# Gated linear attention feeding a mixture of experts: the order of the first loads and TensorE's first products

## The chip, the cores and the metric

The kernel runs on one core of one Trainium2 chip. The metric is the device time of one execution in microseconds (us), smaller is better. Engines are named as the profile names them: PE is TensorE's matmul, PEld its weight load, DVE is VectorE, ACT ScalarE, POOL GpSimd, and SP the engine that only issues transfers; a trailing q (SPq, ACTq) is an engine's sequencer, where the issue of a transfer is shown.

## The reference

The inputs are q, k, v and f_logit of shape (4, 8, 768, 48) in fp32. Attention is a gated recurrence per batch and head, and its rows go through a router to one of eight experts:

```python
f = 1.0 / (1.0 + np.exp(-f_logit))
for t in range(S):
    state = f[:, :, t, :, None] * state + np.einsum('bhd,bhe->bhde', k[:, :, t], v[:, :, t])
    y[:, :, t] = np.einsum('bhd,bhde->bhe', q[:, :, t], state)
x = y.transpose(0, 2, 1, 3).reshape(B * S, H * D)      # 3072 rows of 384
logits = x @ w_gate; e = argmax(logits)                # 8 experts
# the first `capacity` rows of an expert go through relu(x @ w1[e]) @ w2[e],
# scaled by the softmax of their gate
```

## The kernel before, in words

Attention works through 24 chunks of 128 tokens (six for each of the four batches), all eight heads of a chunk at once, heads paired two by two. A chunk n is taken through these steps, named by the function and the line that the profile shows:

- `load` (L205, L210, L216) issues its transfers from SP: "f" for two chunks at once (384 KB), k and q of one chunk (192 KB each, k on partitions 0 to 63, q on 64 to 127), v (192 KB). f, kq and v have 3, 3 and 6 buffers. Only the first half of f's first load is split over SP and ACT (L214), heads 0 to 3 and heads 4 to 7.
- `sig` (L357, ACT) applies the sigmoid to a load of f; for the first load rows 0 to 63 and rows 64 to 127 are done apart.
- `f_in` (L366, PE) transposes f of a chunk, eight transposes per chunk. `decay` (L386, L394, L395, DVE) is a scan backwards over it, `decay_back` (L400, DVE) a scan forwards.
- `kq_pad` (L407, POOL up to chunk 9, then ACT) copies k and q into a padded tile, `kq_in` (L366, PE; L415, DVE) transposes them and multiplies the transposes by the two scans to give kT and qT.
- `scores_pe` (L426, PE), `scores_out` (L432 ACT, L434 POOL) make the masked scores AT; `keys_pe` and `keys_out` (L451, L457) the key rows; `inter` (L468) the part from the state S; `update` (L488), `state` (L502 or, for a first chunk, L500, DVE) and `carry` (L508, POOL) the next state; `values` (L522) the part from the scores; `y_out` (L534) and `rows_pe` (L543) turn the output into rows, and `rows_copy` (L559) and `rows_parts` (L569) put them and their logits into `ring`, a tile of 12 chunks of rows. From slot 7 on, a group's expert choice is ranked and POOL scatters its rows to `disp` in DRAM (L326), one chunk of rows in a slot.

The order on all five engines is the order of emission, written out by hand: `prologue` (L770) takes chunk 0 and the first steps of chunks 1 to 3, and `slot(n)` (L826) then holds, for one n, the scores of chunk n+1, kq_in of n+2, the decay of n+3, the loads of later chunks (`loads_of`, L812) and the values of chunk n. `keep_busy(m)` (L373) is m products of the identity with itself into a PSUM tile that nobody reads; a fp32 product shows as two matmul instructions, a transpose as one. There are 7 of them before the first transposes, 4 before kq_in(0) and 2 before kq_in(1).

`late_constants` (L278) loads the gate weights into `identc` with four transfers of 32-byte pieces, issued by SP behind the load of v for chunk 1. `zero_disp` (L345) writes 393 KB of zeros to `disp`, once for each of two regions, in slots 1 and 3, ahead of any scatter; each scatter must come behind both, since its rows can fall in either.

After attention (from about 150 us) the experts run as dense products (L754, L1015, L1222), each expert's weights loaded during the one before.

Of the kernel before, what the change touches and what calls it, by code (L numbers as in the profile page):

```python
# [9 lines left out]
F32 = mybir.dt.float32  # L10
# [4 lines left out]
AF = mybir.ActivationFunctionType  # L15
# [5 lines left out]
P = 128  # L21
# [8 lines left out]
def kernel(  # L30
# [12 lines left out]
    nc = tc.nc  # L43
    B, H, S, D = q.shape
    N, DM = out.shape
    NE = w_gate.shape[1]
    DF = w1.shape[2]
    NP = H // 2
    HALF = 384
    C = 128  # L50
# [3 lines left out]
    R = 64 + D  # L54
    DT = DM // P
    FT = DF // P
    W = DM + NE + 1
# [4 lines left out]
    RT, RING = 4, 12  # L62
# [20 lines left out]
    psT = ctx.enter_context(tc.tile_pool(name="psT", bufs=2, space=PSUM))  # L83
    psA = ctx.enter_context(tc.tile_pool(name="psA", bufs=2, space=PSUM))
# [5 lines left out]
    ident = const.tile([P, P], F32, name="ident")  # L90
# [81 lines left out]
    actx = ExitStack()  # L172
    apool = actx.enter_context(tc.tile_pool(name="apool", bufs=1))
    abuf = actx.enter_context(tc.tile_pool(name="abuf", bufs=2))
    raw0 = actx.enter_context(tc.tile_pool(name="raw0", bufs=3))
    h0pool = actx.enter_context(tc.tile_pool(name="h0pool", bufs=1))

# [2 lines left out]
    loads, pf, kqp = {}, [], []  # L180
    for nm in ("f", "kq", "v"):
        for i in range(NLOAD[nm]):
            if nm == "v":
                t = apool.tile([P, H, 64], F32, name=f"ld_{nm}{i}")
                nc.gpsimd.memset(t[:, :, D:], 0.0)
            else:
                t = apool.tile([P, H, 2, D], F32, name=f"ld_{nm}{i}")
            loads[nm, i] = t
    for made, nm, n in ((pf, "pf", 2), (kqp, "kqp", 2)):
        for i in range(n):  # L190
            t = apool.tile([P, 2, H, 64], F32, name=f"{nm}{i}")
# [7 lines left out]
    def load(nm, n):  # L199
        if n >= (NT // 2 if nm == "f" else NT):  # L200
            return
        t = loads[nm, n % NLOAD[nm]]
        if nm == "v":
            b, t0 = n // CPB, n % CPB * C
            nc.sync.dma_start(t[:, :, :D], srcs[nm][b, :, t0 : t0 + C, :].rearrange("h p d -> p h d"))  # L205
            return
        t = t.rearrange("t h j d -> t h (j d)")
        if nm == "kq":
            for h, x in enumerate(nm):
                nc.sync.dma_start(t[64 * h : 64 * h + 64], pairs(x, n, C))  # L210
        elif n == 0:
            for h, queue in enumerate((nc.sync, nc.scalar)):
                hs = slice(4 * h, 4 * h + 4)
                queue.dma_start(t[:64, hs], pairs(nm, 0, C)[:, hs])  # L214
        else:
            nc.sync.dma_start(t, pairs(nm, 2 * n, 2 * C))  # L216

    def loaded(nm, n):
        return loads[nm, n % NLOAD[nm]]

    for nm, n in (("f", 0), ("kq", 0), ("kq", 1), ("f", 1), ("kq", 2), ("v", 0), ("f", 2)):
        load(nm, n)
        if (nm, n) == ("kq", 0):
            nc.sync.dma_start(loads["f", 0].rearrange("t h j d -> t h (j d)")[64:], pairs("f", 1, C))
# [5 lines left out]
    for i in range(2):  # L230
        t = apool.tile([P, NP * C], F32, name=f"Suf{i}")
# [21 lines left out]
    for g in range(2):  # L253
        r = slice(64 * g, 64 * g + D)
# [23 lines left out]
    def late_constants():  # L278
        gates_of = w_gate.rearrange("(a b s d) e -> b s d a e", b=2, s=2, d=D)
        for g in range(2):  # L280
            for b in range(2):
                nc.sync.dma_start(identc[64 * g : 64 * g + D, b::2, 2 * D :], gates_of[b, g ^ b])
    ohc = const.tile([P, NE], BF16, name="ohc")
    lt = const.tile([P, NS, NS], F32, name="lt")
    put_off(nc.gpsimd.memset, lt, 1.0)
# [59 lines left out]
    def zero_disp(v):  # L345
        ins = nc.sync.dma_start(
            disp[v * RPE : v * RPE + 2 * P, :].rearrange("(a p) w -> p a w", p=P),
            zero.unsqueeze(1).broadcast_to([P, 2, W]),
        )
        after(ins, pace["ins"], "behind the first loads")  # L350

    def sig(u):
        if u >= NT // 2:
            return
        cuts = (0, 64, P) if u == 0 else (0, P)
        for r0, r1 in zip(cuts, cuts[1:]):
            pace["ins"] = nc.scalar.activation(  # L357
                pf[u % 2][r0:r1, :, :, :D], loaded("f", u)[r0:r1].rearrange("t h j d -> t j h d"), AF.Sigmoid
            ).ins

    def transposes(*dsts):
        for p in range(NP):
            for j in range(2):
                for t, src, h in dsts:
                    r = slice(64 * h, 64 * h + 64)
                    nc.tensor.transpose(  # L366
                        t[:R, p, j::2], src[r, j, 2 * p : 2 * p + 2].rearrange("t s d -> t (s d)")[:, :R], ident[r, r]
                    )
        return [t[:R].rearrange("r p t -> r (p t)") for t, src, h in dsts]

    Fs, Rqs, kTs, qTs = {}, {}, {}, {}

    def keep_busy(m):  # L373
        pw = psA.tile([P, P], F32, name="psA")
        for _ in range(m):
            nc.tensor.matmul(pw, ident, ident, start=True, stop=True)  # L376

    def f_in(*ns):
        made = [(psF.tile([P, NP, C], F32, name="psF"), pf[n // 2 % 2], n % 2) for n in ns]
        for n, F in zip(ns, transposes(*made)):  # L380
            Fs[n] = F

    def decay(n):
# [19 lines left out]
    def kq_pad(n):  # L403
        if n < NT:
            src = loaded("kq", n).rearrange("t h j d -> t j h d")
            if n - 3 < PAD_ACT:
                nc.gpsimd.tensor_copy(kqp[n % 2][:, :, :, :D], src)  # L407
            else:
                nc.scalar.activation(kqp[n % 2][:, :, :, :D], src, AF.Copy)

    def kq_in(n):
        pts = transposes(*((psT.tile([P, NP, C], F32, name="psT"), kqp[n % 2], h) for h in range(2)))
        for nm, pt, by, made in (("kT", pts[0], Sufb[n % 2], kTs), ("qT", pts[1], Rqs.pop(n), qTs)):
            t = abuf.tile([P, NP, C], F32, name=nm, bufs=3)
            nc.vector.tensor_tensor(t[:R].rearrange("r p t -> r (p t)"), pt, by[:R], op=ALU.mult)  # L415
            made[n] = t
# [120 lines left out]
    def rows_pe(n):  # L537
        yT = yTs.pop(n)
        px = psA.tile([P, NP, XW], F32, name="psA")
        for p in range(NP):  # L540
            for t in range(2):
                ts = slice(64 * t, 64 * t + 64)
                m_pe = nc.tensor.matmul(px[ts, p, :], yT[:R, p, ts], identc[:R, p, :], start=True, stop=True)  # L543
        marks[n] = [m_pe]
        return px

    ring = abuf.tile([P, RING, W], F32, name="rows", bufs=1)

    def row_at(n):
        return ring[:, n % RING]  # L550
# [136 lines left out]
    def flush_scatter():  # L687
        if queue:
            n = queue.pop(0)
            late = n >= SPLIT  # L690
            ins = scatter(disp, ri_of.pop(n), row_at(n), NV * RPE - 1, ("disp", "late") if late else ("disp",))
            if not late:
                early_ins[:] = [ins]
# [74 lines left out]
    slots = range(NT + 1)  # L768

    def prologue():  # L770
        keep_busy(7)
        nc.scalar.activation(warm, direv[:, :1], AF.Sigmoid)
        sig(0)
        f_in(0)
        decay_back(0, decay(0))
        kq_pad(0)
        load("kq", 3)
        load("v", 1)
        late_constants()
        keep_busy(4)  # L780
        kq_in(0)
        f_in(1)
        decay_back(1, decay(1))
        kq_pad(1)
        later_ops(put_off_ops)
        keep_busy(2)
        kq_in(1)
        sig(1)
        kq_pad(2)
        pas = scores_pe(0)  # L790
        f_in(2)
        decay_back(2, decay(2))
        scores_out(0, pas)
        pks = keys_pe(0)
        keys_out(0, pks)
        f_in(3)
        load("kq", 4)
        load("v", 2)
        load("kq", 5)
        load("f", 3)  # L800
    ends = {g + m - 1: (g, m) for g, m in GROUPS}

    def rank(g, pool):
# [8 lines left out]
    def loads_of(n):  # L812
        load("v", n + 3)
        if 0 < n < PAD_ACT:
            load("kq", n + 6)
        if n == 0:
            load("f", 4)
        if n == 2:
            nc.sync.dma_start(cap_i, capacity.bitcast(I32).partition_broadcast(P))
        if n in (1, 3):  # L820
            zero_disp(0 if n == 1 else NE)
        for k, at in enumerate(PIECE_LOAD):
            if at == n:
                pieces[k] = weight_piece(wsets[0], 0, raw0, k)

    def slot(n):  # L826
# [17 lines left out]
            choose_first(*half.pop())  # L844
        for g in full:
            choose_sum(*g)
        if n == 1:
            f_in(4)
        if kqn:
            kq_in(n + 2)  # L850
        if n % 2 and fn and n not in (1, 9, 15):
            f_in(n + 3, n + 4)
        if nxt:
            scores_out(n + 1, pas)
        if n == 0:
            sig(2)
        if prev and cur and first(n):
            y_out(n - 1)
# [31 lines left out]
        if nxt:  # L890
            for s in range(SCATTERS.get(n, 2)):
                flush_scatter()
        if fn:
            F = decay(n + 3)
        if prev:
            px = rows_pe(n - 1)
            if tail:
                rows_logits(n - 1, px)
                rows_copy(n - 1, px)
                chosen[n - 1] = choose_one(row_at(n - 1), abuf, tallies[-1][:, 1:2]), 1  # L900
            else:
                rows_copy(n - 1, px)
                rows_parts(n - 1, px)
# [587 lines left out]
```

## Time and profile before

| | us |
|---|---|
| three timed runs | 374.07, 376.09, 376.36 (median 376.09) |
| the profiled execution | 375.17 |
| its span, first to last instruction | 373.40 |
| around the span | 1.77 |
| mean granted TensorE clock of the span | 0.990 |

The span is the part that the views below cut up. A row of a timeline or of the chain has a start, a duration and an instruction group; "[0.34 <-PE psT L366]" is the idle time of that engine just before it, and what ended it. The durations of matmuls overlap, since their ends are modelled; in the chain each has only its own share.

### The profile page before, as it was taken

The numbers are of one execution on the slowest core, as the hardware profiler recorded it, in microseconds if no ns is written. First come the engines' busy times: TensorE is split into PE (matmuls) and PEld (weight loads), VectorE is DVE, ScalarE is ACT, GpSimd is POOL, SyncE is SP. The second block draws the span as 40 slices with busy tenths as digits, with TensorE's granted clock in tenths as the row PEclk, the third lists the DMA queues.
The fourth block names the chain that finished last, engine by engine and source line by source line (L and its number), as shares of the span: only waits on it lengthen the run. The fifth ranks groups of instructions, "written<-read, shape, count | busy, mean of one in ns | idle before, by whom it ended". The sixth has DMA issues, their size and how long they took to land.

```text
span 373.4 us, 10082 instructions
## 1 busy us (share of the span) xinstructions
PE 362.1 (97%) x3895; PEld 340.8 (91%) x3895; DVE 247.8 (66%) x533; ACT 223.8 (60%) x458; POOL 166.5 (45%) x275
## 2 busy tenths in 40 slices
PE   8999999999899999999999999999999999999993
PEld 7999898888787889999899999999999999999993
DVE  4898988979687866753676296857757665570300
ACT  3356677877586763255477475759578586583310
POOL 6665556675757675235613702127117244144012
PEclk9999999999899999999999999999999999999997
DMA  8999999999997432476696979799797997721001
GB/s 153 187 177 224 205 207 227 256 214 226 213 227 164 130 114 105 133 237 204 191 239 188 286 196 242 212 187 319 169 204 247 172 208 253 129 94 52 14 23 40
DMA packets 111351, 67.86 MB, mean 182 GB/s; under 512 B 93646, under 2 KB 105844, under 8 KB 111296
## 3 DMA queue, kind: packets, MB, share of 16 engines
q1 hardware_dynamic: 107504, 57.09, 69.1%
q0 software_dynamic: 3520, 9.97, 7.7%
q8 instruction: 32, 0.52, 0.6%
q14 instruction: 23, 0.19, 0.2%
q10 hardware_dynamic: 272, 0.10, 0.1%
HBM read 49.46 MB, written 11.43 MB: 163 GB/s over the span
## 4 chain that ended last, share of the span: by engine, by line
PE 84%; issue 8%; ACT 3%; POOL 2%; DVE 1%; POOLq 1%; ACTq 0%
PE psM L1222 15%; PE psA L754 9%; PE psM L1015 9%; PE psT L754 9%; PE psM L754 7%; PE psA L426 6%; PE psY L522 6%; PE psA L543 5%; PE psT L366 4%; PE psY L468 3%; PE psA L488 3%; PE psT L451 3%; PE psF L366 2%; POOL out_dram L326 2%; PE psA L376 2%
## 5 line engine op out<-in xcount | busy, mean ns | idle before, releaser
L326 POOL DMA_INDIRECT out_dram<-yo,g_ti x30 | 31.3, 1042 | 55.6 <-ACT yo L1019 31.7
L434 POOL TENSOR_SCALAR_AFFINE_SELECT AT<-AT 128x512 f32<-128x512 f32 x48 | 29.4, 637 | 23.3 <-ACT AT L432 23.2
L1015 PE MATMUL psM<-w2h,hh 128*128 128x384 f32 (+2 forms) x112 | 37.5, 340 | 0.0
L1015 PE MATMUL psM<-w2l,hh 128*128 128x384 f32 (+2 forms) x112 | 37.3, 338 | 0.0
L1015 PE MATMUL psM<-w2h,hl 128*128 128x384 f32 (+2 forms) x112 | 37.2, 338 | 0.0
L135 ACT ACTIVATE w2h<-raw 128x768 fp32r<-128x768 f32 x32 | 27.0, 844 | 11.2 <-DMA raw<-in_moe_w_dram 11.2
L1222 PE MATMUL psM<-hh,w2h 128*128 128x440 f32 (+3 forms) x96 | 33.7, 351 | 0.0
L1222 PE MATMUL psM<-hh,w2l 128*128 128x440 f32 (+3 forms) x96 | 33.7, 351 | 0.0
L1222 PE MATMUL psM<-hl,w2h 128*128 128x440 f32 (+3 forms) x96 | 33.6, 350 | 0.0
L144 DVE TENSOR_TENSOR w2l<-raw,w2h 128x768 fp32r<-128x768 f32 x28 | 27.8, 994 | 7.7 <-ACT w2h L135 6.9
L386 DVE TENSOR_TENSOR_SCAN Suf<-psF,direv 112x511 f32<-112x511 f32 x24 | 29.1, 1212 | 4.5 <-PE psF L366 4.5
L432 ACT ACTIVATE AT<-psA 128x512 f32<-128x512 f32 x48 | 26.4, 612 | 8.9 <-PE psA L426 5.6
L1242 POOL COPY yo<-yq 128x384 uint16<-128x384 uint16 (+4 forms) x16 | 11.9, 790 | 40.1 <-DMA yq<-yp 38.2
L426 PE MATMUL psA<-qT,kT 48*128 48x128 f32 x384 | 29.4, 293 | 0.0
L400 DVE TENSOR_TENSOR_SCAN Rq<-psF,d 112x512 f32<-112x512 f32 x24 | 29.4, 1223 | 0.0
L326 POOL DMA_INDIRECT disp<-rows,ri x24 | 24.8, 1034 | 9.5 <-issue 4.3
L144 DVE TENSOR_TENSOR w1l<-raw,w1h 128x1024 fp32r<-128x1024 f32 x21 | 26.5, 1269 | 2.9 <-ACT w1h L135 2.6
L761 DVE SCALAR_TENSOR_TENSOR hl<-psA,hh 128x224 fp32r<-128x224 f32 (+8 forms) x26 | 14.2, 547 | 21.3 <-ACT hh L760 19.3
L559 ACT ACTIVATE rows<-psA 128x384 f32<-128x384 f32 x24 | 11.8, 491 | 26.0 <-PE psA L543 19.6
L522 PE MATMUL psY<-AT,ld_v 128*48 128x128 f32 (+1 forms) x384 | 26.9, 278 | 0.0
L426 PEld LDWEIGHTS psA<-qT,kT 48*128 48x128 f32 x384 | 25.8, 201 | 0.5 <-issue 0.5
L135 ACT ACTIVATE w1h<-raw 128x1024 fp32r<-128x1024 f32 x24 | 24.8, 1060 | 1.9 <-DMA raw<-in_moe_w_dram 1.9
(253 smaller groups left out, 1041.7 us busy)
## 6 DMA issues: line engine op xcount, KB each, us to landing
raw<-in_moe_w_dram SPq DMA_DIRECT2D x24, 512.0 KB
raw<-in_moe_w_dram SPq DMA_DIRECT2D x32, 384.0 KB
ld_kq<-in_k_dram SPq DMA_DIRECT2D x24, 192.0 KB
ld_kq<-in_q_dram SPq DMA_DIRECT2D x24, 192.0 KB
ld_v<-in_v_dram SPq DMA_DIRECT2D x24, 192.0 KB
ld_f<-in_f_logit_dram SPq DMA_DIRECT2D x11, 384.0 KB
xg<-disp SPq DMA_DIRECT2D x6, 589.5 KB
xg<-disp SPq DMA_DIRECT2D x3, 393.0 KB
```

Source lines behind the costliest of these rows:

```text
L135: return nc.scalar.activation(hi, raw, AF.Copy)
L144: engine.tensor_tensor(lo[cs], raw[cs], hi[cs].bitcast(F32), op=ALU.subtract)
L326: ins = nc.gpsimd.indirect_dma_start(out=dst, out_offset=bass.IndirectOffsetOnAxis(ap=idx, axis=0), in_=rows, in_offset=None, bounds_check ...
L386: nc.vector.tensor_tensor_scan(out=_view(Suf[:R], m - 1, [[-1, m]]), data0=_view(F, m, [[-1, m]]), data1=_view(direv[:R], m - 1, [[-1, m]] ...
L400: nc.vector.tensor_tensor_scan(out=Rq[:R], data0=F, data1=d1[:R], initial=0.0, op0=ALU.mult, op1=ALU.max)
L426: nc.tensor.matmul(pas[s][:, p], kTs[n][r, p], qTs[n][r, p], start=True, stop=True)
L432: nc.scalar.activation(AT[:, s], pas[s], AF.Copy)
L434: nc.gpsimd.affine_select(AT[:, s], AT[:, s], pattern=[[0, NP], [1, C]], compare_op=ALU.is_ge, fill=0.0, base=0, channel_multiplier=-1)
L522: nc.tensor.matmul(py[b][64 * g : 64 * g + m, a, :], vt[:, 2 * p + s, :m], AT[:, s, p, :], start=(first(n) and a == 0), stop=(a == NP // 2 ...
L754: nc.tensor.matmul(ph[:, :T], a[:, c, fs], x[:, c, :T], start=(n == 0), stop=(n == 3 * DT - 1))
L1015: nc.tensor.matmul(py[:n], x[:, ks], a[:, ft], start=(ft == 0 and m == 0), stop=(ft == FT - 1 and m == 2))
L1222: nc.tensor.matmul(pys[c][:, :T], a[:, ft, cs], x[:, :T], start=(ft == 0 and n == 0), stop=(ft == FT - 1 and n == 2))
```

## The change

It reserves the tile `ring` earlier, fills 128 x 128 of it with ones on DVE (`hot`) and multiplies that in `keep_busy` instead of the identity, with 8 products at the start in place of 7. Beside the eight transposes of f_in(0), which read partitions 0 to 63, eight more read the ones on partitions 64 to 127 into another PSUM tile. The first sigmoid is cut in two by heads, kq_pad(0) by partitions (k, then q), and kq_in(0) transposes k first and q after it, not in turns. Of the loads, f of chunks 4 and 5 is issued behind k and q of chunk 3, f of chunks 6 and 7 ahead of k and q of chunk 5, the gate weights are issued by ACT, and the two zero_disp move from slots 1 and 3 to slots 4 and 6. The sigmoid for chunks 4 and 5 moves from slot 0 to slot 1, and f_in(4) within slot 1 from ahead of kq_in(3) to behind rows_pe(0).

```diff
+    ring = abuf.tile([P, RING, W], F32, name="rows", bufs=1)
+    hot = ring[:, 0, :P]
+    nc.vector.memset(hot, 1.0)
...
-    for nm, n in (("f", 0), ("kq", 0), ("kq", 1), ("f", 1), ("kq", 2), ("v", 0), ("f", 2)):
+    for nm, n in (("f", 0), ("kq", 0), ("kq", 1), ("f", 1), ("kq", 2), ("v", 0)):
...
-                nc.sync.dma_start(identc[64 * g : 64 * g + D, b::2, 2 * D :], gates_of[b, g ^ b])
+                nc.scalar.dma_start(identc[64 * g : 64 * g + D, b::2, 2 * D :], gates_of[b, g ^ b])
...
-        cuts = (0, 64, P) if u == 0 else (0, P)
-        for r0, r1 in zip(cuts, cuts[1:]):
+        cuts = ((0, 64, 0, H // 2), (0, 64, H // 2, H), (64, P, 0, H)) if u == 0 else ((0, P, 0, H),)
+        for r0, r1, h0, h1 in cuts:
...
+                if beside is not None:
+                    nc.tensor.transpose(beside[:R, p, j::2], hot[64:, :R], ident[64:, 64:])
...
-            nc.tensor.matmul(pw, ident, ident, start=True, stop=True)
+            nc.tensor.matmul(pw, hot, hot, start=True, stop=True)
...
+        beside = None if ns[0] else psA.tile([P, NP, C], F32, name="psA")
+        for n, F in zip(ns, transposes(*made, beside=beside)):
...
-                nc.gpsimd.tensor_copy(kqp[n % 2][:, :, :, :D], src)
+                for r in (slice(0, 64), slice(64, P)) if n == 0 else (slice(0, P),):
+                    nc.gpsimd.tensor_copy(kqp[n % 2][r, :, :, :D], src[r])
...
+        pts = transposes(*made) if n else [transposes(one)[0] for one in made]
...
-        keep_busy(7)
+        keep_busy(8)
...
         load("kq", 3)
+        load("f", 2)
         load("v", 1)
...
+        load("f", 3)
         load("kq", 5)
-        load("f", 3)
...
-        if n in (1, 3):
-            zero_disp(0 if n == 1 else NE)
+        if n in (4, 6):
+            zero_disp(0 if n == 4 else NE)
...
-        if n == 1:
-            f_in(4)
...
-        if n == 0:
+        if n == 1:
             sig(2)
...
+        if n == 1:
+            px = rows_pe(0)
+            f_in(4)
         if fn:
             F = decay(n + 3)
         if prev:
-            px = rows_pe(n - 1)
+            px = px if n == 1 else rows_pe(n - 1)
```

## Rows read from the trace of the kernel before

**Rows 1.** Windows by stage: us from the span's start, length, busy by engine, PEclk, DMA share, GB/s.

```profile
1.83:18.00 16.17, 16.15 (x141) 15.18 (x143) 10.97 (x21) 5.94 (x10) 10.29 (x56) 1.00 1.19 195
18.00:45.60 27.60, 27.60 (x619) 25.12 (x617) 25.01 (x44) 16.64 (x45) 15.34 (x27) 1.00 1.02 197
45.60:150.00 104.40, 100.72 (x1939) 88.93 (x1934) 84.41 (x209) 71.45 (x174) 66.36 (x107) 0.98 0.88 188
150.00:340.00 190.00, 190.00 (x1053) 184.30 (x1052) 122.27 (x250) 123.36 (x218) 68.79 (x72) 1.00 0.78 203
```

**Rows 2.** Chain that ended last, prologue: start us, us, what.

```profile
1.83 3.35 PE psA L376 x14
...
11.32 1.03 PE psT L366 x16
12.36 1.81 PE psA L426 x16
...
20.30 0.95 PE psA L426 x15
```

**Rows 3.** Windows, a stretch late in attention.

```profile
99.90:103.30 3.40, 3.40 (x47) 3.40 (x44) 2.52 (x5) 1.21 (x3) 2.12 (x4) 0.50 1.08 206
```

**Rows 4.** Chain in that stretch and in the next slot.

```profile
102.04 1.57 PE psY L522 x16
...
107.28 0.88 PE psY L522 x16
```

**Rows 5.** Timeline of DVE, 0 to 28 us: start, duration, line, idle before.

```profile
9.35 0.69 DVE L415 TENSOR_TENSOR kT<-psT,Suf 112x512 f32<-112x512 f32 x1 [0.34 <-PE psT L366]
...
15.05 1.22 DVE L386 TENSOR_TENSOR_SCAN Suf<-psF,direv 112x511 f32<-112x511 f32 x1 [0.64 <-PE psF L366]
...
18.41 0.69 DVE L415 TENSOR_TENSOR kT<-psT,Suf 112x512 f32<-112x512 f32 x1 [0.67 <-PE psT L366]
...
23.93 1.21 DVE L386 TENSOR_TENSOR_SCAN Suf<-psF,direv 112x511 f32<-112x511 f32 x1
...
27.16 0.69 DVE L415 TENSOR_TENSOR kT<-psT,Suf 112x512 f32<-112x512 f32 x1 [0.54 <-PE psT L366]
```

**Rows 6.** Timeline of ACT: the first and the third sigmoid.

```profile
4.22 0.84 ACT L357 ACTIVATE pf<-ld_f 64x768 f32<-64x768 f32 x1 [1.15 <-DMA ld_f<-in_f_logit_dram]
...
11.67 0.84 ACT L357 ACTIVATE pf<-ld_f 128x768 f32<-128x768 f32 x1 [2.90 <-DMA ld_f<-in_f_logit_dram]
```

**Rows 7.** Timeline of SP: issues of the gate weights and of later loads.

```profile
14.54 3.40 SPq L282 DMA_DIRECT2D identc<-in_moe_w_gate_dram  x4
...
18.69 0.63 SPq L210 DMA_DIRECT2D ld_kq<-in_q_dram  x1
...
28.08 0.63 SPq L210 DMA_DIRECT2D ld_kq<-in_q_dram  x1
...
54.09 1.01 SPq L210 DMA_DIRECT2D ld_kq<-in_q_dram  x1
```

**Rows 8.** Windows, behind the issue of the gate weights.

```profile
18.00:19.75 1.75, 1.75 (x43) 1.60 (x39) 1.33 (x3) 1.32 (x3) 1.22 (x2) 1.00 0.25 33
```

**Rows 9.** Timeline of POOL: copies of kq, then slots 7 and 8.

```profile
22.66 0.83 POOL L407 COPY kqp<-ld_kq 128x768 f32<-128x768 f32 x1 [1.33 <-DMA ld_kq<-in_q_dram]
...
33.70 0.83 POOL L407 COPY kqp<-ld_kq 128x768 f32<-128x768 f32 x1 [4.18 <-DMA ld_kq<-in_q_dram]
...
53.84 1.19 POOL L326 DMA_INDIRECT disp<-rows,ri  x1 [0.38 <-issue]
56.20 1.22 POOL L434 TENSOR_SCALAR_AFFINE_SELECT AT<-AT 128x512 f32<-128x512 f32 x2 [1.17 <-ACT AT L432]
57.56 0.51 POOL L508 TENSOR_TENSOR S<-U,pendall 112x192 f32<-112x192 f32 x1
```

**Rows 10.** Timeline of PE: rows of chunk 0, and inter of chunk 9.

```profile
23.17 0.89 PE L543 MATMUL psA<-identc,yT 112*64 112x104 f32 x15
...
60.56 0.67 PE L468 MATMUL psY<-qT,S 48*64 48x128 f32 x16
```

More of the change, by code (lines that the diff above doesn't have):

```diff
@@ L354, in sig, with transposes @@
             return
-        cuts = (0, 64, P) if u == 0 else (0, P)
-        for r0, r1 in zip(cuts, cuts[1:]):
+        cuts = ((0, 64, 0, H // 2), (0, 64, H // 2, H), (64, P, 0, H)) if u == 0 else ((0, P, 0, H),)
+        for r0, r1, h0, h1 in cuts:
             pace["ins"] = nc.scalar.activation(
-                pf[u % 2][r0:r1, :, :, :D], loaded("f", u)[r0:r1].rearrange("t h j d -> t j h d"), AF.Sigmoid
+                pf[u % 2][r0:r1, :, h0:h1, :D],
+                loaded("f", u)[r0:r1, h0:h1].rearrange("t h j d -> t j h d"),
+                AF.Sigmoid,
             ).ins
-    def transposes(*dsts):
+    def transposes(*dsts, beside=None):
         for p in range(NP):
@@ L375, in keep_busy @@
         for _ in range(m):
-            nc.tensor.matmul(pw, ident, ident, start=True, stop=True)
+            nc.tensor.matmul(pw, hot, hot, start=True, stop=True)
     def f_in(*ns):
         made = [(psF.tile([P, NP, C], F32, name="psF"), pf[n // 2 % 2], n % 2) for n in ns]
-        for n, F in zip(ns, transposes(*made)):
+        beside = None if ns[0] else psA.tile([P, NP, C], F32, name="psA")
+        for n, F in zip(ns, transposes(*made, beside=beside)):
             Fs[n] = F
@@ L411, in kq_in @@
     def kq_in(n):
-        pts = transposes(*((psT.tile([P, NP, C], F32, name="psT"), kqp[n % 2], h) for h in range(2)))
+        made = [(psT.tile([P, NP, C], F32, name="psT"), kqp[n % 2], h) for h in range(2)]
+        pts = transposes(*made) if n else [transposes(one)[0] for one in made]
         for nm, pt, by, made in (("kT", pts[0], Sufb[n % 2], kTs), ("qT", pts[1], Rqs.pop(n), qTs)):
@@ L545, in rows_pe @@
         return px
-    ring = abuf.tile([P, RING, W], F32, name="rows", bufs=1)
     def row_at(n):
```

## The prediction

> **What bounds the kernel now.** I began with the span cut into stages [rows 1], to see on which engine time can be won at all. From 150 to 340 us PE has no idle time, from 45.6 to 150 us it lacks 3.7 of 104.4 us, and from 18.0 to 45.6 us it lacks nothing, while DVE is busy 25.0 of those 27.6 us. So time is won only where PE is slow or made to wait, and what is early at the end of the prologue is early at the end of the span, unless something in attention takes it back.
>
> Then the chain of waits, in its first pieces [rows 2]. It runs on PE from 1.83 us on almost without a gap, but not at one speed: the 16 score products take 1.81 us at 12.36 and 0.95 us at 20.30. That is a factor of two, so PE runs at the lower of its two levels, 1.2 GHz, until about 18 us and at 2.4 GHz after it. The granted clock of the windows reads 1.00 in the prologue all the same [rows 1], so there the durations must be read instead. Where that column does show a fall, 0.50 from 99.90 to 103.30 us [rows 3], the same stretching goes with it: 1.57 us for the values products against 0.88 in the next slot [rows 4]. What PE did before 18 us was 14 matmul instructions on the identity, transposes of 64 partitions, more identity products, more transposes, and scores.
>
> Third, DVE's timeline, because a PE twice as fast would soon wait for it. From 9.01 us, where DVE begins to wait for the first kT, to the kT of chunk 2 at 18.41 it waits for PE three times, 0.34, 0.64 and 0.67 us [rows 5]; else it is busy. So in the prologue the two engines are nearly level: PE alone could save half of the 5.6 us from 12.36 to 18, some 2.8 us, but DVE's chain can give only its waits and an earlier start.
>
> **The change part by part.**
>
> *Start, clock and the first chain.* The tile of ones needs one DVE memset where the identity keeps the first product waiting until 1.83 us [rows 2]. The start moves to about 1.2 us (an estimate: DVE's memsets begin before 1 us), and 16 instructions at 3.35/14 = 0.24 us end near 5.05. The first sigmoid begins at 4.22 for want of data and takes 0.84 us [rows 6]; in halves of about 0.5 us the transposes of heads 0 to 3 can run at 4.8 and those of heads 4 to 7 at 5.2. By that the first scan starts 0.15 us earlier at the low level and 0.55 at the high one; I take 0.4. The eight transposes beside lie on the other 64 partitions; sixteen in turns take 1.03 us [rows 2], so they cost at most 0.2. The k half of kq_pad(0) starts at k's own landing, which ends the wait of 0.34; it costs POOL a second copy of 0.83 us, hidden in a stretch where POOL is busy 10.3 of 16.2 us [rows 1], and 0.8 late if it were not. If the clock rises early, the waits of 0.64 and 0.67 go too: 0.4 + 0.34 + 0.64 + 0.67 = 2.05 us off DVE's chain, less than PE could give, so 2.05 is the term. If it stays low, 0.15 + 0.34 = 0.5 us is left. Will it rise early? In the new order PE works from about 1.2 to about 8 us, longer without a pause and, in the first transposes, on all 128 partitions, which the stretch before did not. I take early as likely, not sure. Once up it can fall again, as at 99.90 [rows 3], because at the high level PE has long pauses in a prologue that DVE paces; that would leave something between 0.5 and 2.05.
>
> The Trainium skill (TensorE: Matmul & The Clock Gate, Part 4: PE-mode transpose) says that transposes do not count as PE activity in the way products do. The trace does not contradict it: a stretch full of transposes stayed low [rows 2]. By that rule the transposes beside would do nothing, and a clock that stays low, the first rival, gets likelier.
>
> *f_in(4) behind rows_pe(0).* The scan of chunk 4 starts at 23.93 without a wait [rows 5], and the row products of chunk 0 end on PE at 24.06 [rows 10]. Transposes behind them end near 24.6, so the scan is 0.7 us late. DVE then waits 0.54 us before the kT at 27.16 [rows 5], which absorbs most: 0 to 0.7 lost, taken as 0.15.
>
> *Gate weights on ACT, f behind kq.* SP is held from 14.54 to 17.94 us by the four issues [rows 7], and in 18.00 to 19.75 the transfers' share is 0.25 [rows 8] against 1.19 over the prologue [rows 1]. Without this about 1.75 x (1 - 0.25/1.19) = 1.4 us of transfer time comes back. On ACT the issues stand before the sigmoid at 11.67, ahead of which ACT waits 2.90 us for data [rows 6]; at 3.40 us for the four this sigmoid is up to 0.5 us late, and behind it wait f_in(2) and the scan at 15.05 [rows 5]. In the new order that scan is due near 13.5 and the sigmoid ends by 13.0: cost 0, at most 0.5. The loads that come earlier feed copies that wait for them 1.33 and 4.18 us [rows 9], but PE did not wait there [rows 1], so they gain nothing by themselves and only keep ahead of a PE that is 2 us earlier. The f load behind kq of chunk 3 has its sigmoid one slot later: 0.
>
> The Trainium skill (DMA: Bandwidth & Descriptors, Issuing engines are not separate DMA queues) says that transfers from different issuers share the same 16 engines, so that only issue time is saved. Here issue time left those engines nearly empty [rows 8], so the rule alone would call this edit small and the row calls it 1.4 us of transfers; in the sum both are 0.
>
> *zero_disp in slots 4 and 6.* This edit adds a wait. The second one is issued behind the loads of slot 6, of which the last is k and q of chunk 12, away at 55.10 us [rows 7]. It comes 1.4 us earlier for the time regained and about 1.9 us for its own 393 KB at some 200 GB/s no longer ahead of it: issued near 51.8, away by 52.6. Its landing is not shown. Nearest rows: the q of chunk 4, away at 19.32 into empty queues, is used at 22.66, 3.3 us later; that of chunk 6, away at 28.71 into full ones, at 33.70, 5.0 us later [rows 7, 9]. So the zeros land at 55.9 to 57.6. The first scatter is due at 53.84 - 1.9 = 51.9 and must wait for them, and behind it on POOL stand the mask of slot 8 and its carry: 1.19 + 1.22 + 0.51 = 2.9 us [rows 9]. The state that inter(9) reads is then ready at 58.8 to 60.5; inter(9), now at 60.56 [rows 10], is due at 58.7. Price 0.1 to 1.8 us; I take 0.6, nearer to the lower end because PE has idle time of its own in that stage [rows 1] in which a wait can vanish.
>
> Sum: -2.05 + 0.15 + 0 + 0.6 = -1.3 us. Against the profiled execution (span 373.40 and 1.77 around it) that is 375.17 - 1.3 = 373.9. That execution lies 0.92 us under the median of the timed runs but above the fastest of them; the mean of all four is 375.42, and 375.42 - 1.3 = 374.1 is my figure.
>
> **The rivals.**
>
> *The clock stays low until about 18 us*, and the change only orders things anew. For it: 16 us of nearly unbroken work did not raise it sooner [rows 2]. Against it: the new stretch is denser and starts earlier. 0.5 - 0.15 gained, and the zeros 0 to 0.5 us late for a PE that has not moved, 0.2 lost: 375.42 - 0.15 = 375.3.
>
> *The clock rises early and does not fall at 99.90.* The fall costs up to half of 3.40 us, 1.7 [rows 3]. When all is 2 us shifted it may not recur. For it: one timed run, 374.07, is 2 us under the other two, as if it had lacked this fall; against it: the stretch before the fall is thin on PE for reasons that the change does not touch. 374.1 - 1.7 = 372.4.
>
> *The zeros hold POOL.* Slower than before if they land so late that all 1.9 us are given back: carry at 60.6, so landing after 57.7. If SP does not gain the 1.9 us and the backlog costs 5.6, they land at 55.1 - 1.4 + 0.8 + 5.6 = 60.1, the carry ends at 63.0 and PE, due at 58.7, loses 4.3 us: 375.42 - 1.9 + 4.3 = 377.8. For it: full queues, where one load took 5.0 us [rows 9]. Against it: fewer bytes lie ahead of the zeros than lay ahead of slot 6's loads before.
>
> **How the numbers follow.** Forecast 0.52, clock low 0.22, no late fall 0.13, zeros holding POOL 0.13. The time is the forecast's, 374.1. For 8 in 10 I go down past the third case, with 2.05 - 0.15 and 1.7 us off 375.42 at best, to 371.9, and up to 377.0, which takes in the second case and most of the fourth. One per cent, 3.8 us, is about what a measurement of this kernel can tell from no change. Faster by more means under 372.3: nearly half of the third case and a little of the first, 0.10. Slower by more means over 379.8: 0.04. Within: 0.86.
>
> **What would show it.** Right: identity-like products at half their old duration before 11 us; the waits before the scan of chunk 2 and the kT of chunk 2 gone, and that kT near 16.4 instead of 18.41; no hole in the transfers at 18 us; a POOL wait of 4 to 6 us before the first scatter, with inter(9) under 2 us late against the shift. Wrong: score products of 1.8 us in the prologue again; a scan of chunk 4 that waits over 1 us; first scores of slot 1 less than 1 us earlier than 20.30; or a first scatter that starts without a wait.

## The result, and the profile after

The changed kernel takes 379.72 us (median of 6 runs, 379.0 to 380.37), the kernel before 375.66 beside it (6 runs, 373.8 to 376.36): a ratio of 1.0119, 95% interval 1.009 to 1.0148. The forecast was 374.1 in a range to 377.0. What came is the side of the fourth rival, the zeros that hold POOL. A ratio here leaves out runs that lie more than 1.5% above the fastest of their kernel, and is not the quotient of the medians beside it.

The profiled execution after took 379.82 us, with a span of 378.1 (373.4 before). Lines of the kernel are numbered anew in it: L376 of before is L383, L426 is L436, L522 is L532, L508 is L518, L326 is L329, L346 is L349.

**The prologue gained more than I had put down, and kept none of it.** PE's timeline after; the rows answer to [rows 2]:

```profile
5.88 1.25 PE L383 MATMUL psA<-rows 128*128 128x128 f32 x8
...
11.34 1.11 PE L436 MATMUL psA<-qT,kT 48*128 48x128 f32 x16
...
21.51 0.58 PE L498 MATMUL psA<-ld_v,kn 128*64 128x48 f32 x15 [1.16 <-DMA ld_v<-in_v_dram]
```

The first score products take 1.11 us in this view, where the same view of before shows:

```profile
6.21 2.07 PE L376 MATMUL psA<-ident 128*128 128x128 f32 x8
...
12.14 2.02 PE L426 MATMUL psA<-qT,kT 48*128 48x128 f32 x16
```

So by the durations PE ran at its higher level, 2.4 GHz, from about 6 us on, and not from 18. DVE's timeline after, which answers to [rows 5]:

```profile
5.98 1.22 DVE L394 TENSOR_TENSOR_SCAN Suf<-psF,direv 112x511 f32<-112x511 f32 x1 [3.36 <-PE psA L375]
...
13.55 1.21 DVE L394 TENSOR_TENSOR_SCAN Suf<-psF,direv 112x511 f32<-112x511 f32 x1
...
16.16 0.67 DVE L425 TENSOR_TENSOR kT<-psT,Suf 112x512 f32<-112x512 f32 x1
...
23.50 1.22 DVE L394 TENSOR_TENSOR_SCAN Suf<-psF,direv 112x511 f32<-112x511 f32 x1 [0.87 <-PE psF L371]
```

The waits of 0.34, 0.64 and 0.67 us are gone, and the kT of chunk 2 comes at 16.16 instead of 18.41. The values products of chunk 0 start at 16.00 (18.76 before), 2.76 us earlier. One slot later the lead is 0.43 us, and at chunk 4 it is gone (table below): at 21.51 PE waits 1.16 us for v of chunk 1, as shown, and POOL waits 4.38 us for k and q of chunk 4, up to 23.41, where before it waited 1.33 us up to 22.66 [rows 9]:

```profile
23.41 0.83 POOL L416 COPY kqp<-ld_kq 128x768 f32<-128x768 f32 x1 [4.38 <-DMA ld_kq<-in_q_dram]
```

Engines that are earlier found transfers that were not. The hole of [rows 8] is filled:

```profile
18.00:19.75 1.75, 1.55 (x36) 1.29 (x36) 1.72 (x4) 1.75 (x6) 1.04 (x2) 1.00 1.22 169
```

Its share went from 0.25 to 1.22. Yet the total rate over the first two stages of [rows 1] did not rise; windows after, by stage:

```profile
1.83:18.00 16.17, 14.58 (x200) 12.82 (x201) 12.68 (x25) 6.61 (x13) 12.42 (x60) 1.00 1.19 190
18.00:45.60 27.60, 25.71 (x564) 22.98 (x563) 23.21 (x40) 15.95 (x43) 13.77 (x25) 1.00 1.13 182
45.60:60.00 14.40, 14.10 (x324) 12.88 (x322) 13.32 (x28) 11.32 (x30) 4.20 (x7) 1.00 1.17 230
60.00:65.00 5.00, 0.53 (x18) 0.39 (x15) 1.50 (x3) 2.29 (x5) 2.50 (x4) 0.91 1.13 218
65.00:70.00 5.00, 4.57 (x67) 4.11 (x69) 1.26 (x2) 0.00 (x0) 3.76 (x8) 0.50 1.17 260
70.00:75.00 5.00, 5.00 (x104) 4.50 (x102) 4.02 (x12) 4.17 (x10) 2.14 (x3) 0.90 1.11 247
75.00:150.00 75.00, 73.42 (x1415) 64.63 (x1412) 61.64 (x154) 52.23 (x128) 52.42 (x85) 1.00 0.74 174
```

190 and 182 GB/s stand against 195 and 197 [rows 1]. In the second stage, in which the hole lies, before moved its two transfers of zeros as well, 2 x 393 KB or 28 GB/s over 27.6 us; without them its loads moved some 169 GB/s (an estimate, 197 - 28), so the loads after did go faster there, by about 13. Up to 18 us there is no such reason, and the loads went no faster.

**The loss is at 60 us.** PE is busy 0.53 of the 5 us from 60 to 65, and the granted clock is 0.50 in the 5 us behind. POOL's timeline after, against [rows 9]:

```profile
62.48 1.19 POOL L329 DMA_INDIRECT disp<-rows,ri  x1 [8.88 <-DMA disp<-zero]
63.69 1.22 POOL L444 TENSOR_SCALAR_AFFINE_SELECT AT<-AT 128x512 f32<-128x512 f32 x2
64.88 0.50 POOL L518 TENSOR_TENSOR S<-U,pendall 112x192 f32<-112x192 f32 x1
```

The first scatter waits 8.88 us for the second transfer of zeros; mask and carry stand behind it, and PE's products on the state stand behind the carry. PE's timeline, against [rows 10]:

```profile
65.43 1.13 PE L478 MATMUL psY<-qT,S 48*64 48x128 f32 x16 [4.90 <-POOL S L518]
...
68.41 1.61 PE L553 MATMUL psA<-identc,yT 112*64 112x104 f32 x15
69.65 1.77 PE L532 MATMUL psY<-AT,ld_v 128*48 128x128 f32 x16
```

Inter(9) starts at 65.43 and not at 60.56, after 4.90 us of waiting. Behind it everything is stretched: the row products take 1.61 us, where 0.89 is the rule [rows 10]. From values(8) to values(9) it is 12.03 us, 5.58 before. The zeros themselves, in SP's timeline (against [rows 7]) and in the chain that ended last:

```profile
44.71 1.78 SPq L349 DMA_DIRECT2D disp<-zero  x1
...
53.20 1.31 SPq L213 DMA_DIRECT2D ld_kq<-in_q_dram  x1
54.60 2.08 SPq L349 DMA_DIRECT2D disp<-zero  x1
```

```profile
54.60 6.94 DMA disp<-zero
...
62.48 1.19 POOL disp L329
```

Its issue begins at 54.60 and ends at 56.68, and it landed at 61.54: 4.9 us after the issue ended, inside the 3.3 to 5.0 that I had taken. The issue itself was due at 51.8 and began 2.8 us later, and then it took 2.08 us. SP's waits from 20 to 57 us (in total, times, longest) name ACT for this:

```profile
SPq L349 <- ACT AT L442: 3.4, 2, 1.7
```

That does not hold. Of ACT's work, the transfers of zeros are ordered only behind the last sigmoid issued ahead of them, in slot 4 the one at 37.36 and in slot 6 this one, which ended 6.5 us before SP came to the zeros:

```profile
47.28 0.87 ACT L360 ACTIVATE pf<-ld_f 128x768 f32<-128x768 f32 x1
```

So the view names what ACT happened to finish while the issue ran. The two issues took 1.78 and 2.08 us after, 0.57 and 1.66 us in the same slots of e2, 0.56 and 0.57 us in slots 1 and 3 (e1); what makes some of them long is open.

**Where it stood at each slot.** Starts of the values products (L522, L532) of chunk n in PE's timeline, us; e1 to h2 are runs of the next section, h1 is the kernel before itself:

| n | before | after | e1 | e2 | e3 | g1 | h1 | h2 |
|---|---|---|---|---|---|---|---|---|
| 0 | 18.76 | 16.00 | 18.45 | 18.62 | 16.00 | 16.00 | 16.29 | 16.19 |
| 1 | 23.82 | 23.39 | 24.17 | 23.68 | 23.12 | 23.11 | 22.74 | 22.23 |
| 4 | 38.58 | 38.70 | 38.82 | 38.71 | 38.45 | 38.14 | 39.02 | 37.49 |
| 8 | 57.48 | 57.62 | 57.73 | 57.88 | 57.36 | 57.06 | 57.93 | 56.41 |
| 9 | 63.06 | 69.65 | 62.92 | 69.08 | 67.87 | 62.25 | 64.24 | 69.13 |
| 15 | 94.52 | 101.17 | 94.23 | 100.34 | 97.91 | 92.29 | 94.28 | 99.80 |
| 16 | 101.66 | 105.77 | 99.59 | 107.31 | 102.51 | 96.89 | 98.88 | 104.40 |
| 20 | 123.82 | 127.36 | 119.63 | 127.95 | 122.32 | 116.92 | 118.66 | 124.19 |
| 21 | 128.72 | 132.26 | 128.50 | 133.19 | 127.26 | 126.17 | 128.33 | 129.09 |
| 23 | 142.91 | 146.53 | 143.05 | 146.82 | 140.89 | 141.21 | 142.36 | 142.71 |

At chunk 9 the changed kernel is 6.59 us behind. It wins 2.54 back from 15 to 16, since the fall of [rows 3] does not come (7.14 and 4.60 us), and stands 3.62 behind at chunk 23; the span ends 4.7 behind. That fall belongs to one execution and not to the kernel: h1, the same code as before, does not have it either (4.60 us from 15 to 16).

### The profile page after: what moved, and what is told of

Read it like the earlier page. It is cut to its first block, busy times and chain, and to the rows that moved or that the text cites. A ratio compares the mean times of both kernels' runs of the same rounds, so it can differ in the third digit from the quotient of the medians.

```text
span 378.1 us, 10109 instructions
## 1 busy us (share of the span) xinstructions
PE 359.9 (95%) x3905; PEld 338.1 (89%) x3905; DVE 247.4 (65%) x534; ACT 224.0 (59%) x459; POOL 168.9 (45%) x276
## 4 chain that ended last, share of the span: by engine, by line
PE 70%; issue 10%; DMA 8%; POOL 4%; ACT 3%; SPq 2%; DVE 1%; POOLq 1%; ACTq 0%
PE psM L1232 14%; PE psA L762 9%; PE psT L762 8%; PE psM L1025 8%; PE psM L762 5%; PE psA L553 5%; PE psY L532 4%; PE psA L436 3%; DMA ld_kq<-in_q_dram 3%; PE psY L478 2%; PE psA L498 2%; PE psT L371 2%; DMA ld_v<-in_v_dram 2%; PE psT L461 2%; DMA disp<-zero 2%
## 5 line engine op out<-in xcount | busy, mean ns | idle before, releaser
L329 POOL DMA_INDIRECT out_dram<-yo,g_ti x30 | 32.6, 1086 | 49.6 <-ACT yo L1029 30.4
L329 POOL DMA_INDIRECT disp<-rows,ri x24 | 24.8, 1034 | 17.6 <-DMA disp<-zero 8.9
L144 DVE TENSOR_TENSOR w1l<-raw,w1h 128x1024 fp32r<-128x1024 f32 x21 | 27.3, 1312 | 1.2 <-ACT w1h L135 0.9
L436 PE MATMUL psA<-qT,kT 48*128 48x128 f32 x384 | 27.5, 280 | 0.0
L532 PE MATMUL psY<-AT,ld_v 128*48 128x128 f32 (+1 forms) x384 | 26.6, 277 | 0.0
L436 PEld LDWEIGHTS psA<-qT,kT 48*128 48x128 f32 x384 | 24.1, 189 | 0.7 <-issue 0.5
```

Of the source, the lines that this page charges most:

```text
L144: engine.tensor_tensor(lo[cs], raw[cs], hi[cs].bitcast(F32), op=ALU.subtract)
L329: ins = nc.gpsimd.indirect_dma_start(out=dst, out_offset=bass.IndirectOffsetOnAxis(ap=idx, axis=0), in_=rows, in_offset=None, bounds_check ...
L436: nc.tensor.matmul(pas[s][:, p], kTs[n][r, p], qTs[n][r, p], start=True, stop=True)
L532: nc.tensor.matmul(py[b][64 * g : 64 * g + m, a, :], vt[:, 2 * p + s, :m], AT[:, s, p, :], start=(first(n) and a == 0), stop=(a == NP // 2 ...
```

## The experiments

Expectations speak of the kernel after as "after", of the one before as "before". Each ratio is to runs of before that were timed in the same series; e1 to e4 are one series, c1 and e5 to e7 another, g1 to g4 a third, h1 and h2 a fourth.

**e1 and e2: the zeros alone, taken away and put in.** e1 is the kernel after with the zeros back:

```diff
-        if n in (4, 6):
-            zero_disp(0 if n == 4 else NE)
+        if n in (1, 3):
+            zero_disp(0 if n == 1 else NE)
```

> The changed kernel with the two zero_disp back in slots 1 and 3. Theory Z (the zeros hold POOL, and through the state PE): the 8.88 us wait of POOL before the first scatter and the 4.90 us wait of PE before inter(9) go, no granted clock of 0.5 at 64 to 71 us; between the values products of slots 8 and 9 the changed kernel takes 12.03 us and the one before 5.58, so 379.7 - 6.45 = 373.3 us, up to 375.8 if the clock falls late in attention again, which cost 2.5 there. Theory L (the loss is made by the loads that come late in the first slots): 378 us or more.

Measured: 373.85 us, ratio 0.9959, interval 0.9917 to 1.0001. The first scatter goes at 54.09 without a wait for zeros, and PE's products on the state of chunk 9 have none either:

```profile
54.09 1.19 POOL L329 DMA_INDIRECT disp<-rows,ri  x1 [0.38 <-issue]
```

e2 is the kernel before with that one edit the other way round, zeros in slots 4 and 6.

> The kernel before with nothing changed but the two zero_disp, in slots 4 and 6. Theory Z: 5 to 6.5 us slower than before, 380.7 to 382.2, or 378.2 if the late fall of the clock goes away as it did with the whole change. Theory L: within 1 us of before, 374.7 to 376.7.

Measured: 378.35 us, ratio 1.0144, interval 1.0095 to 1.0192. POOL's and PE's timelines:

```profile
62.25 1.20 POOL L326 DMA_INDIRECT disp<-rows,ri  x1 [8.38 <-DMA disp<-zero]
...
65.22 0.86 PE L468 MATMUL psY<-qT,S 48*64 48x128 f32 x16 [4.41 <-POOL S L508]
```

The wait is that of the kernel after to half a microsecond, in a kernel with nothing else of the change. Slot 8 to 9 is 11.20 us there and 5.19 in e1. So the zeros alone make the loss in slot 9, shown from both sides, and in this series the loss at the end. That e2 came near the 378.2 named for a kernel without the late fall is luck: e2's profile has such a fall, a granted clock of 0.50 from 106.5 to 109.9 us, and 6.97 us from 15 to 16.

**g1: the zeros two slots earlier.** The kernel after with the zeros in slots 2 and 4 (the line above with 2, 4 and 2).

> The kernel after, with its two transfers of zeros issued in slots 2 and 4 instead of 4 and 6. Theory Z (what counts is only when the second transfer is issued, since it lands about 7 us after its issue begins: 54.60 to 61.55 in the kernel after): the second is issued near 44.7, where the kernel after issues its first, and lands by 52, before the first scatter is due at 52 to 54; no scatter waits for it, slot 8 to 9 takes 5.2 to 6.0 us, and the time is that of the version with the zeros in slots 1 and 3, within 0.5%: a ratio to before of 0.993 to 1.001. Rival Y (any transfer of zeros behind the prologue's slots delays the loads and the scatters beside it): slot 8 to 9 takes over 8 us, and the ratio is 1.005 to 1.013.

Measured: 373.06 us, ratio 0.9971, interval 0.9924 to 1.0018. SP and POOL:

```profile
45.51 0.58 SPq L349 DMA_DIRECT2D disp<-zero  x1
...
53.42 1.19 POOL L329 DMA_INDIRECT disp<-rows,ri  x1 [0.38 <-issue]
```

Issued at 45.51, the second transfer is no longer waited for; slot 8 to 9 is 5.19 us. The moment of the issue decides, not that zeros move in attention: the rival falls.

**e3 and g3: the wait without the clock.** The kernel after, with PE kept on products of ones while it waits:

```diff
+        if n == 9:
+            keep_busy(14)
         if cur:
             inter(n)
```

> The changed kernel with 14 products of the tile of ones put on PE ahead of inter(9), where it waits 4.90 us for the state; about 28 instructions of 0.14 us, 3.9 us, so they fit in the wait. If the fall of the clock after that wait costs what the stretched rows show (values of slot 9 at 65.43 + 4.2 against 2.5 us after inter, 1.7 us), the granted clock stays 1.00 there and the time is 378.0. If it costs nothing of its own, 379.7; if the products delay the slot, 380 or more.

Measured: 373.80 us, ratio 1.0035, interval 0.9982 to 1.0087. PE's timeline and the window behind:

```profile
60.66 3.39 PE L383 MATMUL psA<-rows 128*128 128x128 f32 x28 [0.38 <-ACT AT L442]
65.52 0.67 PE L478 MATMUL psY<-qT,S 48*64 48x128 f32 x16 [1.48 <-POOL S L518]
...
67.21 0.89 PE L553 MATMUL psA<-identc,yT 112*64 112x104 f32 x15
```

```profile
65.00:70.00 5.00, 4.48 (x102) 4.07 (x104) 2.46 (x5) 1.84 (x6) 4.58 (x9) 1.00 1.11 253
```

The products on the state come no sooner (65.52), but the granted clock stays 1.00, the row products take 0.89 us again, and slot 8 to 9 is 10.51 us instead of 12.03: by this pair, which is not of one series, the fall costs 1.5 us of the 6.45 in that slot. The time came 4.2 us under the 378.0 named, far more than the clock's share: e3's profile has neither the late fall (4.60 us from 15 to 16) nor a wait at the first gather (h1, below), and its slots 13 to 15 take 15.1 us where those of the kernel after take 16.6. The same kernel again, beside the kernel after (g4):

> The kernel after with fourteen products of ones ahead of the products that wait for the scatter in slot 9, on the chip of the kernel after beside it. Theory H (the wait of TensorE costs 4.9 us, and the clock that falls in it a further 1.5 to 1.8): it stays slower than before by 1.0 to 1.4% less 0.4 to 0.5%, a ratio to before of 1.005 to 1.010, and lies 1.0 to 3.0 us under the kernel after. Rival W (the wait alone costs what is lost; the clock costs nothing that is left at the end): within 0.7 us of the kernel after.

Measured: 374.29 us, ratio 1.0019, interval 0.997 to 1.0069; slot 8 to 9 10.31 us, against 11.65 in g4. In the slot 1.3 us are saved, but the medians are only 0.36 us apart (374.65 for g4), which is nearer to the rival's expectation. That the clock's share reaches the end is not shown.

**e4 and e5: what takes the prologue's gain.** e4 is e1 with the loads of f in their old order (f of chunks 4 and 5 ahead of kq of chunk 3, f of 6 and 7 behind kq of 5).

> The changed kernel with the zeros back in slots 1 and 3 and also the loads of f in the old order (f of chunks 4 and 5 before k and q of chunk 3, f of chunks 6 and 7 behind k and q of chunk 5). Theory G (the new order of loads makes v of chunk 1 and k and q of chunk 4 late, which gives back 2.3 of the 2.8 us that the prologue wins): 2 us below the kernel with only the zeros back, about 371.5. Rival (the transfers are the bound in the first slots in any order): within 0.5 us of it, about 373.3.

Measured: 374.01 us, ratio 0.9988, interval 0.9936 to 1.0039. Values(0) starts at 16.67 and values(1) at 24.07, so the lead is lost in the same slot with the old order: the order of the loads is not what takes it. e5 is e1 without three loads (its output differs: chunk 4's k and q and chunks 6 and 7's f are those of other chunks):

```diff
-        load("kq", 4)
         load("v", 2)
-        load("f", 3)
         load("kq", 5)
```

> The changed kernel with the zeros back in slots 1 and 3, and without the loads of k and q of chunk 4 and of f of chunks 6 and 7 (0.77 MB, about 3.9 us of transfers); these chunks use what lies in the buffers, so their rows differ from the reference's. Theory T (transfers bound the first slots, and so give back what the early clock wins): values(1) about 4.6 us behind values(0), near 20.7 instead of 23.4 to 24.2, and the time 2 to 2.8 us under the kernel with only the zeros back (373.85): 371 to 372. Rival (PE and DVE take the time of slot 1 themselves, f_in(4) behind rows_pe(0) among it): values(1) stays at 23 or later and the time within 0.7 us of it.

Measured: 373.71 us, ratio 0.9944, interval 0.9908 to 0.9979. That is 1.7 us or more above the 371 to 372 expected, and values(1) came at 22.33, not near 20.7. Values(4) starts at 36.98, 1.6 us ahead of before, where no kernel of the table is ahead by more than 1.1. But slot 0 to 1 is 6.59 us with the light loads, inside what the changed kernel shows with all of them (7.39 after, 6.04 in h2). That transfers hold that stretch is not shown by this run; the waits at 21.51 and 23.41 above are what speaks for it.

**e6 and e7: the ones alone, the transposes beside alone.** e6 is the kernel before with the tile of ones and keep_busy(8) on it; e7 is the kernel before with the eight transposes beside (of the identity, no ones).

> The kernel before with the tile of ones in keep_busy and 8 products at the start, and nothing else. If the earlier start and the additional product raise the clock, score products of chunk 0 take about 1.0 us instead of 1.81 and the first values product starts near 16.5; if the transposes beside are needed for it, 1.8 us and 18.3 or later. The time tells little, 374 to 376.

> The kernel before with eight transposes on partitions 64 to 127 beside those of f_in(0), reading the identity there, and nothing else. If the transposes beside raise the clock, score products of chunk 0 take about 1.0 us; if the earlier start and the longer first stretch are needed, 1.8 us as before and a first values product at 18.3 or later.

Measured in a single execution each: 375.94 and 375.86 us, with score products of 1.11 us in both and values(0) at 15.86 and 16.36. Values(4) starts at 39.84 and 39.19, behind before's 38.58: the lead goes without the new loads as well. I first read this as either edit raising the clock by itself. h1 (below) takes that reading away.

**c1, g4: the kernel after, again.** Same code, measured in two more series.

> The changed kernel as it is, on this call's chip beside the kernel before, as a control for the run with products ahead of inter(9). If those products saved what a held clock saves, this kernel is about 1.2% above before (its first comparison) while that one was 0.35% above: 377.5 to 380. If the two chips differ instead, about 374.

> The kernel after, once more, as the measure for the runs beside it: a ratio to before of 1.008 to 1.015, and slot 8 to 9 of 11.5 to 12.5 us.

Measured: c1 379.59 us, ratio 1.0116 (1.0079 to 1.0152); g4 374.65 us, ratio 1.0035 (0.9991 to 1.0079), though slot 8 to 9 takes 12.33 and 11.65 us. The loss at slot 9 is the same, the loss at the end is not. And g2, e1 once more beside g4:

> The kernel after with the zeros in slots 1 and 3 again, once more, on the chip of the runs beside it. If the rest of the change is worth something at the end, the ratio to before lies under 0.997 with its whole interval; if what it gains in the prologue is given back by slot 4, as the traces show, the interval holds 0.998 to 1.000. Expected: the second, 0.996 to 1.000.

Measured: 372.59 us, ratio 0.9947, interval 0.9895 to 0.9999: under the 0.996 to 1.000 expected, and no further than before itself lies against its own code (h1, below).

**h1 and h2: the kernel before, profiled beside the kernel after.** Slots 13 to 15 (values(12) to values(15)) take 16.6 us in the profiles before and after and in c1, 16.6 to 16.8 in e5 to e7 and 16.2 in e2, but 15.1 or 15.2 in e1, e3, e4 and g1 to g4; the kernel before had no profile of the second kind.

> The kernel before itself, with a profile taken in the call of the run beside it, and timed as one more kernel against itself (a measure of what the ratio can tell): ratio 0.995 to 1.005. Theory G (the wait for the zeros is partly given back at the gather of the first expert group): where slots 13 to 15 take about 5.0 us each, TensorE of this kernel waits for the gather near 120 us, or loses its clock there, and the ratio of the changed kernel in this call is under 1.008; where these slots take 5.3 to 5.7, it does not wait, and the ratio is 1.009 to 1.014. Rival: no wait for the gather in this kernel and a ratio under 1.008 all the same; then what is given back lies elsewhere.

> The kernel after, beside the kernel before with its profile. Its first scatter waits for the zeros again and slot 8 to 9 takes 11.5 to 12.5 us. Theory G: TensorE does not wait for the gather of the first expert group (it arrives 4 to 6 us later than in the kernel before), and the ratio to before is under 1.008 if slots 13 to 15 take about 5.0 us each, 1.009 to 1.014 if they take 5.3 to 5.7. Rival: the ratio does not go with the length of these slots.

Measured: h1 372.49 us, ratio 0.9947 to its own code (interval 0.9907 to 0.9987); h2 376.22 us, ratio 1.0021 (0.9975 to 1.0068). Slots 13 to 15 take 15.1 us in both. PE's timeline of h1, first in the prologue, then at the first expert group:

```profile
6.17 1.19 PE L376 MATMUL psA<-ident 128*128 128x128 f32 x8
...
11.29 1.11 PE L426 MATMUL psA<-qT,kT 48*128 48x128 f32 x16
...
125.63 0.65 PE L718 MATMUL psF<-ident,xg 128*128 128x128 f32 x2 [3.52 <-DMA xg<-disp]
```

Its chain of waits and its windows there:

```profile
115.75 6.05 DMA disp<-rows,ri
...
121.82 3.76 DMA xg<-disp
```

```profile
120.00:125.00 5.00, 2.10 (x52) 1.79 (x48) 3.99 (x9) 3.04 (x8) 3.18 (x4) 1.00 0.37 100
125.00:130.00 5.00, 4.37 (x52) 3.88 (x53) 1.34 (x5) 0.96 (x3) 1.62 (x3) 0.66 0.42 110
```

h2's PE at the same point, and the issue of that gather on its SP:

```profile
127.56 0.44 PE L726 MATMUL psF<-ident,xg 128*128 128x128 f32 x2
```

```profile
124.02 0.37 SPq L959 DMA_DIRECT2D xg<-disp  x1
```

Two things follow. First, the kernel that is 5.5 us ahead at chunk 20 (118.66 against 124.19) waits 3.52 us for the gather of the first expert group, which waits for a scatter, and its clock falls (0.66 in the next window); the other finds its rows there. At chunk 21 the distance is 0.76 us. That is where most of the lead went in these two profiles, and g1 shows the same wait:

```profile
123.42 0.69 PE L726 MATMUL psF<-ident,xg 128*128 128x128 f32 x2 [3.06 <-DMA xg<-disp]
```

In the profiles before and c1, where slots 13 to 15 take 16.6 us, PE does not wait for this gather, and the loss stays. In e1 and e2 part of it stays: e1 is 8.32 us ahead at chunk 20 and, after 8.87 us for that slot, 4.69 at chunk 21. What makes slots 13 to 15 longer in some executions is open; it comes and goes in one and the same code. How much of the loss is missing in the series of h1 and h2 is not settled either: by the medians h2 is 3.7 us above h1, which is the kernel before itself, and only 1.0 above the other runs of before (375.2).

Second, the kernel before, unchanged, raised its clock as early as the kernel after: 1.11 us for the first score products, values(0) at 16.29. So the early clock is not the change's alone. With the changed start, ten of eleven profiles have values(0) before 16.7 us (e1 has 18.45, at a granted clock of 0.50 from 10.9 to 17.7 us); with the start of before it is one of three (18.76, 18.62, 16.29). The change may make it likelier; that is not shown.

## Why the prediction was wrong, step by step

**Start, clock and the first chain (2.05 off): the mechanism held, its owner and its worth did not.** 2.76 us were gained at values(0), all three waits of [rows 5] went, and the kT of chunk 2 came at 16.16 (16.4 was named). But the table shows 0.12 us lost at chunk 4, where 2.05 were to be kept. The step that failed is that what is early at the end of the prologue is early at the end of the span: attention took it back, most of it in one slot, in which PE and POOL waited for loads that were not earlier. How much of it those loads took is not shown (e5). [Rows 9] showed POOL waiting 1.33 and 4.18 us for loads; I wrote that PE did not wait there, and so that these loads only had to keep ahead. A wait of an engine off the path, hidden by less than the gain, can be the next bound. And h1 shows that the profile of before was one draw: the same code had the early clock too. The Trainium skill's rule (TensorE: Matmul & The Clock Gate, Part 4: PE-mode transpose), which made the low clock likelier, is not decided here: e7 had the early clock with transposes beside, and h1 without.

**f_in(4) (0.15): small, as said.** The scan of chunk 4 waits 0.87 us where I had put 0.7, behind v of chunk 1 on PE, and starts at 23.50 (23.93 before).

**Gate weights and f (0): not contradicted.** The hole closed, and nothing at the end is seen to come of it, though no run has this edit alone. The Trainium skill's rule that issuers share the 16 engines (DMA: Bandwidth & Descriptors, Issuing engines are not separate DMA queues) called the edit small; the trace agrees as to the total, with 190 and 182 GB/s where there were 195 and 197.

**The zeros (0.6): the step that failed.** 6.45 us were lost in slot 9. Of the terms, the landing 3.3 to 5.0 us after the issue was right (4.9), and so was what stands behind on POOL (1.19 + 1.22 + 0.50 = 2.9). Wrong was the issue at 51.8: I moved SP 1.4 us earlier for the transfer time regained and 1.9 us for the zeros no longer ahead. SP was 0.9 us earlier at q of chunk 12 (53.20 against 54.09 in [rows 7]). Of the 1.4 us nothing is to be seen at q of chunk 7, here after and before:

```profile
31.92 0.89 SPq L213 DMA_DIRECT2D ld_kq<-in_q_dram  x1
```

```profile
31.11 0.88 SPq L210 DMA_DIRECT2D ld_kq<-in_q_dram  x1
```

From there to q of chunk 12, with one transfer of zeros less ahead, SP gained 1.7 us, near the 1.9. So the term that failed is the regained transfer time; why it did not reach SP is open. Then the issue took 2.08 us where I had put 0.8, and the zeros landed at 61.54 instead of 57.6 at the latest. Missed altogether was what a PE wait of almost 5 us does to the clock: 1.3 to 1.5 us in the same slot (g3, e3). And I chose 0.6 between 0.1 and 1.8 because a wait could vanish in PE's idle time, where the wait was on the path.

**The rivals.** The fourth had the place and the chain right: landing at 60.1 (61.54 measured), 4.3 us lost on PE (4.90). It still counted 1.9 us of the prologue as kept and left out the clock: 375.42 + 4.9 + 1.5 = 381.8 would have been its figure, less the 2.5 us that the fall of [rows 3] did not take, 379.3. Its chance of 0.13 was too low, for it was enough that one of SP's two gains failed to come and that the issue was long. Of the third, the absent fall came true, but not by the change (h1 lacks it too), and it counted for the wrong sum.

**At the end.** The ratio was 1.0119 and 1.0116 in two series, 1.0035 and 1.0021 in two others. One reason shown is that a kernel that is not late at slot 9 may wait at the first gather instead (h1, g1); that it accounts for the whole difference is not shown. With the zeros early (e1, g1, g2) the rest of the change is worth nothing that these series can tell: 0.9959, 0.9971 and 0.9947, where before against its own code was 0.9947. No version here is shown to beat the kernel before.

## What to carry to other kernels

A transfer that something must wait for is timed by the issue queue it stands in: read from a trace when that queue really gets there, count no gain that the issue times of its other loads do not show, and put it a full landing time (here 7 us from the start of its issue) ahead of its first use. Before counting a prologue's gain to the end, look at the next loads that the engines off the path wait for. Profile the kernel before more than once where its clock is part of the argument, and time it against itself.

## What the runs showed that I had not expected

- One wait of PE of 4.90 us cost a further 1.3 to 1.5 us in its slot (two pairs of profiles): the granted clock was 0.50 from 65 to 70 us, at first under work that was due anyway. Products of ones during the wait kept it at 1.00.
- The clock of the prologue differs between profiles of one and the same code: first score products of 2.02 us in one profile of the kernel before, 1.11 in the other.
- The interval of a kernel against its own code, 0.9907 to 0.9987, left out 1. Half a per cent between two kernels of one series can be nothing here, whatever the interval says.
- A gain of 5.5 us at chunk 20 shrank to 0.76 at chunk 21, at one gather whose scatter took 6.05 us to land (h1).
